# A mixer's second layer in seven block products for eight, with seven accumulators open and its weight sums streamed

## The chip, the core and the metric

The kernel runs on one core of one Trainium2 chip. The core has five engines that run side by side and meet at semaphores: TensorE (PE, matrix products into PSUM), VectorE (DVE), ScalarE (ACT), GpSimd (POOL) and SyncE (SP, which here issues the DMAs). PSUM has eight banks of 128 x 512 fp32; only PE, DVE and ACT reach it here. The metric is device time in microseconds of one execution.

## What is computed

The reference, cut to what matters. The first stage is a causal attention with decay; its output goes, rearranged, into a mixer of two parts.

```python
def _attn_ref(q, k, v, f):              # 8 x 8 heads, 576 tokens, 64 wide
    scores = np.matmul(q, k.transpose(0, 1, 3, 2)) / np.sqrt(64)
    cum = np.cumsum(np.log(np.clip(f, 0.0001, 1.0)), axis=-1)
    scores = np.where(causal, -1e9, scores + cum[:, :, :, None] - cum[:, :, None, :])
    ...
    return np.matmul(attn, v)           # attn: softmax of scores

def _moe_ref(x, U, V, w_ch1, w_ch2):    # x: 8 x 576 x 512
    h = x.transpose(0, 2, 1) @ U @ V
    u = x + h.transpose(0, 2, 1)
    ch = np.maximum(u @ w_ch1, 0.0) @ w_ch2     # 512 -> 2048 -> 512
    return u + ch
```

The two layers of `ch` are most of the arithmetic: 4608 tokens, each through 512 x 2048 and 2048 x 512 weights.

## The kernel before

**Precision.** Every fp32 operand of these layers is held as a high part `h` (rounded to what TensorE multiplies) and a low part `l`, the rest. One product is three matmuls: high by high, low by high, high by low. A matmul has a stationary operand of 128 x 128 (loaded by LDWEIGHTS) and a moving one of up to 512 columns.

**Sweeps.** The 2048 hidden units are 16 chunks of 128. The first sweep goes through attention, mixing and the first six chunks (`NA`), batch by batch; it stores the tokens `u` (to `ud`, high and low) and the sum so far (to `accd`) in HBM. The second sweep takes the other ten chunks (`NB`), whose weights then lie in SBUF: `b1h`, `b1l`, `b2h`, `b2l`. They are read and decoded from raw 64-bit words at the end of the first sweep (`wb_unit`, L976; `decode`, L52: mostly DVE instructions on SBUF).

**Groups.** The second sweep has nine groups of 512 tokens: eight batches and one of the batches' last 64 tokens. Group 0 runs chunk by chunk (`first`, L1034, 12 matmuls of 512 columns; `second`, L1046, 12 matmuls of 512 columns), while the sums of weights and tokens for the rest are made on DVE. Groups 1 to 8 run in five *pairs* of chunks (`pair_of_chunks`, L1151). The first layer of a pair is a 2 x 2 block product (two halves of the 512 model columns, two chunks, two halves of the tokens), done in seven block products for eight, after Strassen and Winograd: `product` (L1143) is six matmuls of 256 columns into a PSUM bank, and DVE forms the sums of products (`plus`, L1167), each reading a bank. The operands are sums too: `weight_sums` (L1089), once, and `token_sums` (L1120, eight DVE instructions of 512 columns per group, from `un`, the next group's tokens) with `token_part` (L1138, ACT the high part, DVE the low).

`relu` (L1029) then makes the hidden units' high part (ACT) and low part (DVE). The second layer is not in block products: `second` adds 3 matmuls of 512 columns to one of four open banks `O` per quarter of the tokens; the last one adds the bank to the group's accumulator in `xn` (L1058) and stores it.

**Order.** In groups 1 to 8 PE and DVE keep the order in which the program is written (`manual_schedule`); the other engines' order comes from a planner that works with estimated times. PE's order is written out so that the second layer of the pair before (`ready`) fills the time in which the first layer's sums are made:

```python
        m5 = product(bank(psF, "F", 5), S1, T1)
        renewed(3)
        plus(s4, m5, s2)
        step()
        go(3)
```

All loads and stores go through SP's queue, in order. Tokens have two buffers (`load_u`, L1020; the next group's 2 MB are asked for at the start of a group). A name in a row of the profile is that of the tile without its number: `M` a bank of the first layer, `O` one of the second, `sum` the tiles of `tmp`, `bh` and `bl` hidden units, `sr` raw weights, `Th` and `Tl` the sums of tokens.

Of the kernel before, what the change touches and what calls it, by code (L numbers as in the profile page):

```python
# [21 lines left out]
P = 128  # L22
# [19 lines left out]
def tile_decay_attention_moe(ctx, tc, qk, v, f, U, V, w1, w2, out):  # L42
# [4 lines left out]
    accd = nc.dram_tensor("accd", (NG, NM, P, DM), F32, kind="Internal").ap()  # L47

# [927 lines left out]
    def wb_unit(i, r):  # L976
        t = stp.tile([P, 1024], I32, tag="raw", name=f"sr{i}{r}")
        if r:
            nc.sync.dma_start(t, w1_src(NA + i))
            h, l = (x[i].rearrange("p c f -> p (c f)") for x in (b1h, b1l))  # L980
        else:
            nc.sync.dma_start(t, w2_src(NA + i))
            h, l = b2h[i], b2l[i]

        a = xn[(B - 3) % NX][:, (2 * i + r) % NM].bitcast(I32)
        decode(t.rearrange("p (n t) -> p n t", t=2), a, h, l, nc.scalar, sub=nc.vector)

# [24 lines left out]

    pool = pools(left, "left")
    up = pool("up", 2)
# [3 lines left out]
    HT = MAIN // 2  # L1018

    def load_u(g):  # L1020
        t = up.tile([P, 2, NDC, MAIN], F32R, tag="u", name=f"u{g}")
        for x in range(2):
            nc.sync.dma_start(t.bitcast(F32)[:, x], ud[g, :, x])
        return t[:, 0], t[:, 1]

    def hidden(name):
        return hp_.tile([P, MAIN], F32R, tag="hh", name=f"bh{name}"), hp_.tile([P, MAIN], F32R, tag="hl", name=f"bl{name}")

    def relu(h, src, cols):  # L1029
        hh, hl = h[0][:, cols], h[1][:, cols]  # L1030
        nc.scalar.activation(hh, src, AF.Relu)  # L1031
        nc.vector.scalar_tensor_tensor(hl, src, 0.0, hh.bitcast(F32), op0=ALU.max, op1=ALU.subtract)

    def first(g, u, i):  # L1034
# [7 lines left out]
        h = hidden(f"{g}_{i}")  # L1042
        relu(h, ps, slice(0, MAIN))
        return h

    def second(z, i, h, x):  # L1046
# [10 lines left out]
        g, o = z["g"], z["acc"][:, x]  # L1057
        nc.vector.tensor_tensor(o, po, o, op=ALU.add)  # L1058
        if g < B:
            nc.sync.dma_start(out[g, P * x : P * x + P], o)  # L1060
        else:
            nc.sync.dma_start(out[2 * x + 1, MAIN:S], o[0:64])
            nc.sync.dma_start(out[2 * x, MAIN:S], o[64:128])
# [6 lines left out]
    for i in range(NB // 2):  # L1070
        blocks = []
        for x in range(3):
# [5 lines left out]
            blocks.append([y.rearrange("p (c f) -> p c f", c=2) for y in pair])  # L1078
        SW.append(blocks)
    Th = sf.tile([P, 4, 2, HT], F32R, tag="uh", name="Th")  # L1080
    Tl = sf.tile([P, 4, 2, HT], F32R, tag="ul", name="Tl")
    tmp = [sf2.tile([P, 2, HT], F32, tag="ost", name=f"sum{x}") for x in range(2)]
    tmp.append(sf.tile([P, 2, HT], F32, tag="TS", name="sum2"))
    tmp = [t[:, y] for t in tmp for y in range(2)]
# [4 lines left out]
    def weight_sums(i, tmp=tmp):  # L1089
        def whole(dst, r, c):  # L1090
            h, l = block(i, r, c)
            nc.vector.tensor_tensor(dst, h.bitcast(F32), l.bitcast(F32), op=ALU.add)

        def diff(dst, x, y, op=ALU.subtract):
            nc.vector.tensor_tensor(dst, x, y, op=op)

        t = [x.rearrange("p (c f) -> p c f", c=2) for x in tmp]
        S1, (S2, S3, S4) = block(i, 1, 0), SW[i]

        def part(dst, src):  # L1100
            split(*dst, src, nc.scalar, nc.vector)

        return [
            lambda: whole(t[0], 1, 0),
            lambda: whole(t[2], 0, 0),
            lambda: diff(t[4], t[2], t[0]),
            lambda: part(S3, t[4]),
            lambda: whole(t[1], 1, 1),
            lambda: diff(t[0], t[0], t[1], ALU.add),
            lambda: part(S1, t[0]),  # L1110
            lambda: diff(t[1], t[0], t[2]),
            lambda: part(S2, t[1]),
            lambda: whole(t[3], 0, 1),
            lambda: diff(t[3], t[3], t[1]),
            lambda: part(S4, t[3]),
        ]

    whole_u = xn[2][:, 0:4].rearrange("p q (c t) -> p q c t", c=2)

    def token_sums(u):  # L1120

        def whole(q):
            c, t = 2 * (q // 2), HT * (q % 2)
            h, l = (x[:, c : c + 2, t : t + HT].bitcast(F32) for x in u)
            nc.vector.tensor_tensor(whole_u[:, q], h, l, op=ALU.add)

        def diff(dst, x, y):
            nc.vector.tensor_tensor(dst, x, y, op=ALU.subtract)

        b11, b12, b21, b22 = (whole_u[:, q] for q in range(4))  # L1130
        return [
            lambda: whole(0), lambda: whole(1),
            lambda: diff(b11, b12, b11), lambda: whole(3),
            lambda: diff(b12, b22, b12), lambda: whole(2),
            lambda: diff(b22, b22, b11), lambda: diff(b21, b21, b22),
        ]

    def token_part(q):  # L1138
        split(Th[:, q], Tl[:, q], whole_u[:, q], nc.scalar, nc.vector)

    T1, T3, T4, T2 = ([x[:, q] for x in (Th, Tl)] for q in range(4))

    def product(ps, a, b):  # L1143
# [5 lines left out]
        return ps  # L1149

    def pair_of_chunks(z, u, i, ready, renew, steps, many):  # L1151

        def go(k):
            for fn in ready[:k]:
                fn()
            del ready[:k]

        def ub(c, t):  # L1160
            return [x[:, 2 * c : 2 * c + 2, HT * t : HT * t + HT] for x in u]

        def bank(pool, tag, k):
            return pool.tile([P, 512], F32, tag=tag, name=f"M{k}_{g}_{i}")[:, 0:HT]

        def plus(dst, ps, other):
            nc.vector.tensor_tensor(dst, ps, other, op=ALU.add)  # L1167

        def step():
            for fn in steps[:many]:  # L1170
                fn()
            del steps[:many]

        def renewed(q):
            if renew:
                token_part(q)

        g = z["g"]
        S1, (S2, S3, S4) = block(i, 1, 0), SW[i]
        h = [hidden(f"{g}_{2 * i + r}") for r in range(2)]  # L1180
        lo, hi = slice(0, HT), slice(HT, MAIN)
        s1, s2, s3, s4, c11, c22 = tmp
        m1 = product(bank(psF, "F", 1), block(i, 0, 0), ub(0, 0))
        nc.scalar.copy(s1, m1)
        m6 = product(bank(psX, "X", 6), S2, T2)
        plus(s2, m6, s1)
        m5 = product(bank(psF, "F", 5), S1, T1)
        renewed(3)
        plus(s4, m5, s2)
        step()  # L1190
        go(3)
        m2 = product(bank(psX, "X", 2), block(i, 0, 1), ub(1, 0))
        plus(c11, m2, s1)
        renewed(0)
        m7 = product(bank(psF, "F", 7), S3, T3)
        plus(c22, m7, s4)
        plus(s3, m7, s2)
        relu(h[0], c11, lo)
        step()
        go(3)  # L1200
        plus(s3, product(bank(psX, "X", 4), block(i, 1, 1), T4), s3)
        relu(h[1], c22, hi)
        renewed(1)
        step()
        plus(s4, product(bank(psX, "X", 3), S4, ub(1, 1)), s4)
# [99 lines left out]
```

## Time and profile before

| | us |
|---|---|
| median of 3 runs (lowest, highest) | 1232.79 (1232.65, 1232.98) |
| the profiled execution | 1233.62 |
| its span, first to last instruction | 1231.8 |
| matmuls O of the second layer in the second sweep, 1080 in all, in the chain of work that ended last | 20% of the span |
| matmuls M of the first layer, groups 1 to 8, in the same chain | 16% |
| DVE busy in 700 to 800 us | 93.08 of 100 |

The profile gives each engine's busy time, the same in stretches, groups of instructions by line of the program, and the chain of work that ended last, followed back from the last instruction. A row of the time line has its start, its duration, the engine, the line, the operation and its tiles; in square brackets stands how long the engine had been idle before it and who ended that. Durations of matmuls are longer than their distance, because they are pipelined: 280 ns each, but some 118 ns from start to start.

### The profile page before, as it was taken

The numbers are of one execution on the slowest core, as the hardware profiler recorded it, in microseconds if no ns is written. First come the engines' busy times: TensorE is split into PE (matmuls) and PEld (weight loads), VectorE is DVE, ScalarE is ACT, GpSimd is POOL, SyncE is SP. The second block draws the span as 40 slices with busy tenths as digits, with TensorE's granted clock in tenths as the row PEclk, the third lists the DMA queues.
The fourth block names the chain that finished last, engine by engine and source line by source line (L and its number), as shares of the span: only waits on it lengthen the run. The fifth ranks groups of instructions, "written<-read, shape, count | busy, mean of one in ns | idle before, by whom it ended". The sixth has DMA issues, their size and how long they took to land.

```text
span 1231.8 us, 21702 instructions
## 1 busy us (share of the span) xinstructions
PE 1201.3 (98%) x7705; PEld 1069.6 (87%) x7705; DVE 896.6 (73%) x2311; ACT 648.9 (53%) x1731; POOL 322.9 (26%) x306
## 2 busy tenths in 40 slices
PE   8999999999999999999999899999999999999998
PEld 6878898988889989989989788888988988898887
DVE  8886888778778777787786799886556555655653
ACT  7787777768767668777675444332122221222211
POOL 3565654444544444444441000000000000000000
PEclk9999999999999999999999999999999999999999
DMA  6546136235325325335342346122130311213010
GB/s 198 151 133 175 51 103 181 76 83 156 89 70 175 106 58 161 99 90 154 87 120 70 115 153 231 35 69 84 55 137 1 137 68 70 103 35 137 1 35 35
DMA packets 67275, 125.85 MB, mean 102 GB/s; under 512 B 7096, under 2 KB 31672, under 8 KB 65120
## 3 DMA queue, kind: packets, MB, share of 16 engines
q1 hardware_dynamic: 67168, 124.47, 33.0%
q8 instruction: 61, 1.00, 0.3%
q14 instruction: 46, 0.38, 0.1%
HBM read 88.66 MB, written 35.78 MB: 101 GB/s over the span
## 4 chain that ended last, share of the span: by engine, by line
PE 83%; DVE 10%; ACT 3%; issue 2%; DMA 1%; POOL 1%; ACTq 0%; DVEq 0%; POOLq 0%
PE O L1054 20%; PE M L1147 16%; PE A L737 10%; PE B L755 9%; PE V L586 5%; PE T L462 4%; PE S L361 3%; PE Hb L1040 2%; PE S L362 2%; PE V L543 1%; PE Tt L646 1%; PE S L358 1%; PE Tu L688 1%; PE St L361 1%; DVE xn L675 1%
## 5 line engine op out<-in xcount | busy, mean ns | idle before, releaser
L1167 DVE TENSOR_TENSOR sum<-M,sum 128x256 f32<-128x256 f32 x280 | 114.7, 422 | 161.0 <-PE M L1147 159.8
L1031 ACT ACTIVATE bh<-sum 128x256 fp32r<-128x256 f32 x160 | 66.8, 419 | 257.5 <-DVE sum L1167 257.5
L390 ACT ACTIVATE P<-S,nm 128x128 f32<-128x128 f32 (+3 forms) x256 | 136.4, 534 | 61.9 <-DVE nm L382 57.6
L382 DVE CUSTOM_DVE_ANT_0 S<-S,mask 128x128 f32<-128x128 f32 (+3 forms) x256 | 125.5, 496 | 45.2 <-PE S L362 36.6
L1054 PE MATMUL O<-b2h,bh 128*128 128x512 f32 x360 | 142.7, 396 | 0.0
L1054 PE MATMUL O<-b2l,bh 128*128 128x512 f32 x360 | 142.2, 395 | 0.0
L1054 PE MATMUL O<-b2h,bl 128*128 128x512 f32 x360 | 141.6, 393 | 0.0
L737 PE MATMUL A<-uh,w1h 128*128 128x256 f32 (+1 forms) x384 | 120.3, 313 | 2.8 <-DVE hl L741 2.8
L737 PE MATMUL A<-ul,w1h 128*128 128x256 f32 (+1 forms) x384 | 113.5, 296 | 0.0
L737 PE MATMUL A<-uh,w1l 128*128 128x256 f32 (+1 forms) x384 | 113.5, 295 | 0.0
L315 POOL CAST G<-qk 64x576 fp32r<-64x576 f32 x52 | 34.9, 672 | 250.0 <-PE St L362 153.7
L755 PE MATMUL B<-w2h,hh 128*128 128x512 f32 x216 | 90.3, 418 | 2.2 <-DVE hl L741 1.2
L462 PE MATMUL T<-ident,P 128*128 128x128 f32 x544 | 87.4, 276 | 0.0
L755 PE MATMUL B<-w2l,hh 128*128 128x512 f32 x216 | 85.0, 394 | 0.0
L755 PE MATMUL B<-w2h,hl 128*128 128x512 f32 x216 | 84.6, 392 | 0.0
L1054 PEld LDWEIGHTS O<-b2l,bh 128*128 128x128 f32 x360 | 67.6, 188 | 16.4
L440 DVE TENSOR_TENSOR PT<-T,PT 128x512 fp32r<-128x512 f32 (+1 forms) x156 | 79.4, 528 | 2.3 <-ACT PT L437 0.6
L586 PE MATMUL V<-PT,VS 128*128 128x448 f32 (+2 forms) x416 | 79.6, 333 | 0.0
L1054 PEld LDWEIGHTS O<-b2h,bl 128*128 128x128 f32 x360 | 67.9, 189 | 11.2
L1054 PEld LDWEIGHTS O<-b2h,bh 128*128 128x128 f32 x360 | 67.9, 189 | 10.6
L737 PEld LDWEIGHTS A<-uh,w1h 128*128 128x128 f32 x384 | 72.9, 190 | 4.5 <-DVE hl L741 4.3
L331 POOL TENSOR_TENSOR G<-qk,G 64x576 fp32r<-64x576 f32 x52 | 74.5, 1433 | 8.5 <-ACT G L315 7.1
(230 smaller groups left out, 3420.5 us busy)
## 6 DMA issues: line engine op xcount, KB each, us to landing
qk<-in_qk_dram SPq DMA_DIRECT2D x104, 288.0 KB
u<-ud SPq DMA_DIRECT2D x16, 1024.0 KB
sr<-in_w_dram SPq DMA_DIRECT2D x20, 512.0 KB
vr<-in_v_dram SPq DMA_DIRECT2D x32, 256.0 KB
accd<-ost SPq DMA_DIRECT2D x32, 256.0 KB
xn<-accd SPq DMA_DIRECT2D x8, 1024.0 KB
out_dram<-xn SPq DMA_DIRECT2D x32, 256.0 KB
ud<-uh SPq DMA_DIRECT2D x7, 1024.0 KB
```

Of the source, the lines that this page charges most:

```text
L331: em.tensor_tensor(g[own, 1, cols], q[own], gf[own, 0, cols], op=ALU.subtract)
L382: nc.vector.tensor_tensor_reduce(ps[:, :w], ps[:, :w], mask[:, 512 - w : 512], scale=-SCALE, scalar=3.0e38, op0=ALU.add, op1=ALU.min, accu ...
L390: nc.scalar.activation(pt, ps[:, :w], AF.Exp, bias=z["nm"][:, col : col + 1], scale=-1.0, accum_out=z["sm"][:, col : col + 1])
L440: defer(2, lambda: nc.vector.tensor_tensor(dstl, src, dsth.bitcast(F32), op=ALU.subtract))
L462: nc.tensor.transpose(tp[:, P * x : P * x + P], z["P"][j][i][:, P * c : P * c + P], ident)
L586: nc.tensor.matmul(pv[:, X0 + lo : X0 + S], VS[:, c, j], pt[:, j, OC[c] + lo - P * c : OC[c] + S - P * c], start=x == 0 and c == 0, stop=F ...
L737: nc.tensor.matmul(ps[:, :nt], wt[:, fc, c], ut[:, c, sl], start=m == 0, stop=m == 3 * NDC - 1)
L755: nc.tensor.matmul(ps, ht[:, fc, P * x : P * x + P], wt[:, fc], start=fc == 0 and m == 0, stop=fc == NA - 1 and m == 2,)
L1031: nc.scalar.activation(hh, src, AF.Relu)
L1054: nc.tensor.matmul(po, ht[:, P * x : P * x + P], wt_[i], start=k == 0 and m == 0, stop=k == NB - 1 and m == 2)
L1147: nc.tensor.matmul(ps, a[x][:, c], b[y][:, c], start=m == 0, stop=m == 5)
L1167: nc.vector.tensor_tensor(dst, ps, other, op=ALU.add)
```

## The change

- **Second layer.** For a pair it too becomes a 2 x 2 block product (two chunks, two halves of the 512 output columns, two halves of the tokens) in seven block products: `product2`, six matmuls of 256 columns. Each product index has an accumulator of its own, open over the five pairs of a group: seven PSUM banks. The sums of products are formed once per group, in `drain`.
- **First layer.** One bank (`FA`) is left for it. A *step* is two products in the two halves of the bank; ACT copies the bank to SBUF (`mc`), and DVE forms the sums from there. The hidden units' sums (`middle`, `last_sum`, `plain_part`) are new, as operands of the second layer.
- **Weights.** The sums of the second layer's weights are made on POOL with ACT during the decoding (`weight_sums2`), stored in HBM (`twd`), and three of four are loaded again for each pair (`load_t`); the fourth is put over a part of `b2h`, `b2l`.
- **Moved.** From group 1 on the token sums and half of the token low parts run on POOL; sums for the first layer's pairs 3 and 4 run on POOL, pair 4 in group 1. Tokens have one buffer `un` and three further tiles (`direct`) for the blocks that are used as they are. They are loaded at pair 1, `direct` in the last pair. ACT too keeps the program's order in groups 1 to 8.

The core of the diff:

```diff
+    twd = nc.dram_tensor("twd", (NB // 2, 4, P, DM), F32, kind="Internal").ap()
...
         decode(t.rearrange("p (n t) -> p n t", t=2), a, h, l, nc.scalar, sub=nc.vector)
+        if i % 2 and not r:
+            weight_sums2(i // 2)
...
+    def weight_sums2(i):
+        eng = nc.gpsimd
+        rows = xn[(B - 2) % NX]
+        w11, w12, w22, w21 = (rows[:, x // 2, 256 * (x % 2) : 256 * (x % 2) + 256] for x in range(4))
...
+        whole(w11, 1, 1)
+        whole(w12, 1, 2)
+        eng.tensor_tensor(w11, w12, w11, op=ALU.subtract)
+        whole(w22, 2, 2)
+        eng.tensor_tensor(w12, w22, w12, op=ALU.subtract)
+        eng.tensor_tensor(w22, w11, w22, op=ALU.subtract)
+        whole(w21, 2, 1)
+        eng.tensor_tensor(w21, w21, w22, op=ALU.add)
+        for x, src in enumerate((w11, w12, w22, w21)):
+            t = rows[:, 2 + x % 2]
+            r = t.bitcast(F32R)
+            split(r[:, 0:256], r[:, 256:512], src, nc.scalar, eng)
+            nc.sync.dma_start(twd[i, x], t)
...
+    def load_t(i, key):
+        nc.sync.dma_start(slots[key].bitcast(F32), twd[i, "1324".index(key)])
+
+    def token_sums(eng):
...
+        for q in range(4):
+            eng.tensor_tensor(whole_u[q], whole_u[q], low_u[q], op=ALU.add)
+        b11, b12, b21, b22 = whole_u
+        diff(low_u[0], b12, b11)
+        diff(low_u[1], b22, b12)
+        diff(low_u[3], b22, low_u[0])
+        diff(low_u[2], b21, low_u[3])
...
+            if i % 2 and i < NB - 1:
+                for fn in weight_sums(i // 2, *((scrap[0:5], nc.vector) if i < 6 else (scrap[5:10], nc.gpsimd))):
+                    fn()
+            if i == NB - 3:
+                token_sums(nc.vector)
...
+    J1, J2 = (1, 6, 5, 2, 7, 4, 3), (4, 1, 5, 6, 7, 2, 3)
...
+        if j == 6:
+            tt(new("2"), m[6], m[1])
+        elif j == 5:
+            tt(new("4"), m[5], s["2"])
+        elif j == 2:
+            tt(new("c11"), m[2], m[1])
+        elif j == 7:
+            tt(new("c22"), m[7], s["4"])
+            tt(new("c21"), m[7], s["2"])
+        elif j == 4:
+            tt(s["c21"], m[4], s["c21"])
+        elif j == 3:
+            tt(new("c12"), m[3], s["4"])
...
+        return act, lambda: tt(k.f[name][1], k.s[key], k.f[name][0].bitcast(F32), ALU.subtract, eng if k.i < NPC - 1 else nc.vector)
+
+    def middle(k):
...
+        def act():
+            nc.scalar.activation(s["c21"], s["c21"], AF.Relu)
+
+        def dve():
+            s["S1"] = fresh()
+            nc.vector.scalar_tensor_tensor(s["S1"], s["c11"], 0.0, s["c21"], op0=ALU.max, op1=ALU.add)
+            s["S2"] = fresh()
+            nc.vector.scalar_tensor_tensor(s["S2"], s["c22"], 0.0, s["S1"], op0=ALU.max, op1=ALU.subtract)
+            nc.vector.scalar_tensor_tensor(s["c21"], s["c22"], 0.0, s["c21"], op0=ALU.max, op1=ALU.subtract)
...
+    AFTER = {
+        2: [(1, lambda k: relu_part(k, "c11", 4))],
+        7: [(1, lambda k: relu_part(k, "c22", 1))],
+        4: [(1, middle), (2, lambda k: plain_part(k, "S1", 5)), (2, lambda k: plain_part(k, "S2", 6)),
+            (2, lambda k: plain_part(k, "c21", 7, nc.gpsimd))],
+        3: [(1, lambda k: relu_part(k, "c12", 2)), (1, last_sum), (2, lambda k: plain_part(k, "S4", 3, nc.gpsimd))],
+    }
...
+    def product2(k, j):
+        ps = acc_ps[j]
+        f, w = k.f[j], operand2(k.i, j)
+        for x in range(2):
+            for m, (a, b) in enumerate(((0, 0), (1, 0), (0, 1))):
+                nc.tensor.matmul(
+                    ps[:, HT * x : HT * x + HT], f[a][:, P * x : P * x + P], w[b],
+                    start=k.i == 0 and m == 0 and x == 0, stop=k.i == NPC - 1 and m == 2, skip_group_check=True,
+                )
+        if j in (4, 6, 7) and (k.n, k.i) != (NG - 1, NPC - 1):
+            load_t((k.i + 1) % NPC, {6: "2", 7: "3", 4: "4"}[j])
+
+    def drain(n, j):
...
+        def rest(blk, t):
+            tt(blk, t, blk, eng=nc.gpsimd)
+
+        if j == 4:
+            tt(C21, ps, C21)
+        elif j == 1:
+            nc.scalar.copy(u, ps)
...
+        elif j == 5:
+            tt(C12, ps, C12)
+            tt(C22, ps, C22)
+        elif j == 6:
+            tt(u6, ps, u)
...
+                tt(C21, ps, C21)
+                tt(C22, ps, C22)
+                rest(C21, u6)
+                rest(C22, u6)
+            store(acc_of(n), (0, 1))
...
+        items = [(n, i, j) for n in range(1, NG) for i in range(NPC) for j in J1]
...
+            batch, items = items[:2], items[2:]
+            if batch:
+                ps = (XA, XB, FB)[s] if s < 3 else FA
+                for x, (n, i, j) in enumerate(batch):
+                    product1(ps[:, HT * x : HT * x + HT], i, j)
...
+                mc = MC[s % 4]
+                nc.scalar.copy(mc, ps)
...
+            todo = [fn(k) for fn, k in later.pop(s, [])]
+            for act, dve in todo:
+                if act:
+                    act()
+            for act, dve in todo:
+                dve()
+            for n, j in drains:
+                drain(n, j)
+            drains = []
+            for n, i, j in batch:
+                if i == NPC - 1 and n + 1 < NG:
+                    if j in direct:
+                        load_direct(order[n + 1], j)
+                    else:
+                        token_part(j, nc.gpsimd)
+                if i == 1 and j == J1[0] and n + 1 < NG:
+                    load_u(order[n + 1])
+                if i == 2 and j == J1[0] and n + 1 < NG:
+                    token_sums(nc.gpsimd)
...
+            for _ in range(2):
+                if queue and queue[0][3] <= s:
+                    n, i, j, _at = queue.pop(0)
+                    product2(pairs[(n, i)], j)
+                    if i == NPC - 1:
+                        drains.append((n, j))
+            s += 1
```

More of the change, by code (lines that the diff above doesn't have):

```diff
@@ L1069, in tile_decay_attention_moe @@
     SW = []
-    for i in range(NB // 2):
+    for i in range(NPC):
         blocks = []
@@ L1077, in tile_decay_attention_moe @@
                 pair = [more[y // 4][:, 256 * (y % 4) : 256 * (y % 4) + 256] for y in (k, k + 1)]
[L1078 removed]
+            blocks.append([halves(y) for y in pair])
         SW.append(blocks)
[L1080 to L1083, printed above, removed]
@@ L1138, in token_part, with one, two, three @@
[L1138 to L1143, printed above, removed]
+            split(*dst, src, nc.scalar, eng)
+        def one():
+            whole(t[0], 1, 0)
+            whole(t[2], 0, 0)
+            diff(t[4], t[2], t[0])
+            whole(t[1], 1, 1)
+        def two():
+            part(S3, t[4])
+            diff(t[0], t[0], t[1], ALU.add)
+        def three():
+            part(S1, t[0])
+            diff(t[1], t[0], t[2])
+            whole(t[3], 0, 1)
@@ new lines, in tile_decay_attention_moe @@
+    TQ = {5: 0, 7: 1, 4: 2, 6: 3}
+    order = [B - 1, *range(B - 2), B, B - 2]
+    load_u(order[1])
+    for j in DIRECT:
+        load_direct(order[1], j)
+    z = {"g": order[0], "acc": xn[1], "po": [None] * NM, "done": [0] * NM}
+    ready = []
+    with tc.manual_schedule(engines={ET.PE}):
+        for i in range(NB):
+            h = first(order[0], cur, i)
+            for fn in ready:
+                fn()
+            ready = [lambda x=x, i=i, h=h: second(z, i, h, x) for x in range(NM)]
+            if i % 2 and i < NB - 1:
+                for fn in weight_sums(i // 2, *((scrap[0:5], nc.vector) if i < 6 else (scrap[5:10], nc.gpsimd))):
+                    fn()
+            if i == NB - 3:
+                token_sums(nc.vector)
@@ L1148, in product @@
                 m += 1
[L1149 to L1205, printed above, removed]
-        renewed(2)
-        go(len(ready))
-        relu(h[1], s3, lo)
-        relu(h[0], s4, hi)
-        step()
-        for r, y in ((0, 0), (0, 1), (1, 2), (1, 3), (1, 0), (1, 1), (0, 2), (0, 3)):
-            ready.append(lambda r=r, y=y: second(z, 2 * i + r, h[r], y))
@@ L1250, in tile_decay_attention_moe, with tt, __init__ @@
-    with tc.manual_schedule(engines={ET.PE}):
-        u, ready = group(0, order[0], cur, [])
-    with tc.manual_schedule(engines={ET.PE, ET.DVE}):
-        for n in range(1, NG):
-            u, ready = group(n, order[n], u, ready)
-        for fn in ready:
-            fn()
+    def tt(dst, x, y, op=ALU.add, eng=nc.vector):
+        eng.tensor_tensor(dst, x, y, op=op)
+    class Pair:
+        def __init__(self, n, i):
+            self.n, self.i = n, i
+            self.m, self.s, self.f = {}, {}, {}
```

275 lines of the change are left out of this document (186 added, 89 removed).

## The prediction

> **What bounds the kernel now.** I read the page's totals first, then the table of stretches, then the chain of work in order of time.
>
> ```profile
> span 1231.8 us, 21702 instructions
> ...
> PE 1201.3 (98%) x7705; PEld 1069.6 (87%) x7705; DVE 896.6 (73%) x2311; ACT 648.9 (53%) x1731; POOL 322.9 (26%) x306
> ...
> POOL 3565654444544444444441000000000000000000
> ```
> ```profile
> 700.00:800.00 100.00, 96.82 (x470) 81.61 (x471) 93.08 (x189) 38.91 (x75) 0.00 (x0) 1.00 0.42 148
> ...
> 900.00:950.00 50.00, 50.00 (x315) 44.94 (x314) 30.01 (x70) 12.44 (x29) 0.00 (x0) 1.00 0.23 85
> ```
> ```profile
> 841.82 2.14 PE M L1147 x18
> 843.96 2.09 PE O L1054 x9
> 846.05 1.42 PE M L1147 x12
> 847.47 2.10 PE O L1054 x9
> 849.57 1.42 PE M L1147 x12
> 850.99 1.40 PE O L1054 x6
> 852.39 2.13 PE M L1147 x18
> ```
>
> TensorE is busy 98% of the span. In the second sweep it never waits: in 900 to 950 us PE is busy all 50 us at full granted clock, while DVE has 30 of 50, ACT 12 and POOL nothing at all. The chain there is a plain alternation of PE groups; nothing else stands in it. One pair of chunks is 42 first-layer matmuls M of 256 columns (2.14 + 1.42 + 1.42 = 4.98 us, 118.5 ns each) and 24 second-layer matmuls O of 512 columns (2.09 + 2.10 + 1.40 = 5.59 us, 233 ns each): 10.57 us, as 841.82 to 852.39 says. Eight groups of five pairs are 40 pairs. So this stage is bound by TensorE alone, and every matmul taken out counts, as long as the other engines can follow. In 700 to 800 us it is different: DVE has 93 of 100 us, and is nearly as full as PE.
>
> **The matmuls.** The second layer of a pair becomes seven products of six matmuls of 256 columns: 42 for 24 of twice the width. No row shows a second-layer matmul of 256 columns; the nearest is M, at 118.5 ns (also with Th and Tl, operands made afresh by ACT and DVE), and half an O is 116.5. I take M's: 42 x 0.1185 = 4.98 us for 5.59. A pair falls from 10.57 to 9.95 us, 0.61 x 40 = **24.4 us less**. The break-even pitch would be 133 ns.
>
> **What DVE must now do.** Per pair it did 7 sums (L1167) and 4 low parts (L1032). It now does 7 sums, 3 low relu parts, 3 instructions of `middle`, 1 of `last_sum` and 2 low parts of `plain_part`: 16, all of 256 columns, and 18 in the last pair of a group.
>
> ```profile
> 1217.29 0.76 DVE L1167 TENSOR_TENSOR sum<-M,sum 128x256 f32<-128x256 f32 x2 [0.29 <-PE M L1147]
> ```
> ```profile
> 716.06 1.29 DVE L69 SCALAR_TENSOR_TENSOR sr<-sr 128x512 f32<-128x512 uint32 x2
> ```
>
> Two in a row take 0.76 us, the single one 0.42, so the pitch is 0.34 us; with 512 columns it is 0.60. 16 x 0.34 = 5.4 of 9.95 us: by time alone DVE has room. So has ACT, with 3.5 copies of a bank (some 0.60 us each) and eight pieces of 256 columns:
>
> ```profile
> L1031 ACT ACTIVATE bh<-sum 128x256 fp32r<-128x256 f32 x160 | 66.8, 419 | 257.5 <-DVE sum L1167 257.5
> ```
>
> 3.5 x 0.60 + 8 x 0.42 = 5.5 us. What changes is where the operands lie. Before, each sum read a PSUM bank. Now ACT copies both products of a step to SBUF (`mc`), and all 16 instructions read two tensors in SBUF. And POOL, idle until now, gets fp32 sums that read SBUF: per group the eight token sums, four low parts (`token_part`), four `rest` of the drain (16 of 512 columns) and two low parts in each of four pairs (8 of 256). The trace has POOL and DVE side by side only in the attention stage:
>
> ```profile
> L630 POOL TENSOR_TENSOR xl<-xn,xh 128x512 fp32r<-128x512 f32 x31 | 40.0, 1291 | 13.6 <-ACT xh L629 12.8
> ...
> L70 POOL TENSOR_TENSOR stg<-stg 128x160 f32<-128x160 f32 x1 | 0.5, 528 | 1.0 <-DMA stg<-in_w_dram 1.0
> ```
> ```profile
> L430 DVE TENSOR_TENSOR sm<-sm x32: 146/826/1416, 15.8 to 655.5; 128x1 f32<-128x1 f32 x32
> ```
> ```profile
> 55.67 1.29 POOL L70 TENSOR_TENSOR stg<-stg 128x512 f32<-128x512 f32 x1 [1.93 <-DVE stg L69]
> ```
> ```profile
> 56.10 0.88 DVE L430 TENSOR_TENSOR sm<-sm 128x1 f32<-128x1 f32 x1
> ```
> ```profile
> 125.52 1.19 DVE L67 SCALAR_TENSOR_TENSOR stg<-stg,xn 128x512 int32<-128x512 int32 x1
> ```
> ```profile
> 37.27 0.45 POOL L632 TENSOR_TENSOR xh<-xn,xh 64x128 fp32r<-64x128 f32 x1
> ```
> ```profile
> 124.78 1.38 POOL L630 TENSOR_TENSOR xl<-xn,xh 128x512 fp32r<-128x512 f32 x1
> 126.23 0.79 POOL L632 TENSOR_TENSOR xh<-xn,xh 64x128 fp32r<-64x128 f32 x1
> ```
> ```profile
> L440 DVE TENSOR_TENSOR PT<-T,PT 128x512 fp32r<-128x512 f32 x52 | 35.6, 685 | 1.1 <-ACT PT L437 0.2
> ```
>
> A POOL sum of 512 columns takes 1.29 us; from 528 ns at 160 columns and 1291 at 512, one of 256 columns is estimated at 0.74. The DVE sum of a single column (L430) takes 0.15 us at best and 0.83 in the median. One instance shows why: it starts at 56.10, while POOL's L70 runs from 55.67 to 56.96, and ends at 56.98. L67, both operands in SBUF, starts at 125.52, lies still until POOL's L630 ends at 126.16 and ends 0.55 later; and POOL's L632, begun at 126.23, waits for it in turn and needs 0.79 us. So the two **take turns, one whole instruction at a time**. Not quite whole: L632 ended 0.31 us after L67 (127.02 against 126.71), though one that waits for nothing takes 0.45 (37.27 us), so some 0.15 us of a POOL instruction can lie beside DVE. L440, with one operand in PSUM, stays at 685 ns in the same stage: such instructions go free, and the old kernel's second sweep was made of them, besides having no POOL work.
>
> [...]
>
> **Where the turns cost time.** A step is two products of each layer, 2.84 us on PE. ACT can copy the bank 1.42 + 0.16 (a matmul's 280 ns less its pitch) after the step's start and needs about 0.60; DVE's 4.6 sums then end at 2.2 + 1.6 = 3.8 us, and ACT takes them up after its next copy, at 2.84 + 2.2 = 5.0. DVE may be late by about 1.2 us; beyond that ACT's next copy is late, the single bank FA is not free, and PE stands. Behind a blocked DVE instruction stand the step's other sums, in order, and the drains.
>
> ```profile
> L177 ACT CAST Th<-xn 128x512 fp32r<-128x512 f32 x22 | 13.6, 617 | 10.8 <-PE M L1147 10.4
> ```
>
> (The copy's 0.60 is from this row of the same size, 617 ns.)
>
> - Pairs 1 and 3: 5.4 + 2 x 0.74 = 6.9 us of 9.95. No cost.
> - Pair 2, with the eight token sums: 5.4 + 1.5 + 8 x 1.29 = 17.2 us (15.7 with 0.15 hidden per turn) for 9.95. Above if all falls into this pair: 7.3 less 1.2 = 6.1 us of stall. Below: spread over pairs 1 to 3 it would be 31.0 of 29.9 us, no stall. I take 3.0, the middle: the sums become ready together, but the last run on into pair 3. **7 groups x 3.0 = 21 us.** Two low parts of the pair before stand behind them in POOL's queue; their product comes late enough that this adds nothing more.
> - Pairs 4 and 0, the boundary: DVE 34 x 0.34 = 11.6, eight drains of 0.60 = 4.8; POOL 2 x 0.74 + 8 x 1.29 = 11.8. With nothing side by side 28.2 us for 19.9; with the drains, which read PSUM, beside POOL and 0.15 hidden per turn, 21.9. Less 1.2: 0.8 to 7.1. I take 2.0, near the lower end because of L440. **7 x 2.0 = 14 us.**
>
> **The front.** In the old kernel DVE decodes the last weights until about 790 us; chunk 9 of b1 has its low part at 781.34 and is read at about 799, b2's of chunk 8 at 789.45 for 799.
>
> ```profile
> 781.34 0.68 DVE L72 TENSOR_TENSOR b1l<-xn,b1h 128x512 fp32r<-128x512 f32 x1
> ...
> 789.45 0.69 DVE L72 TENSOR_TENSOR b2l<-xn,b2h 128x512 fp32r<-128x512 f32 x1
> ```
> ```profile
> 796.00 2.79 PE Hb L1040 x12
> 798.79 2.81 PE O L1054 x12
> ```
>
> Into this stretch `weight_sums2` puts 12 POOL instructions per pair of chunks, and pair 3's sums another 12: 72 x 0.74 = 53 us of POOL, as turns against a DVE that is 93% full and mostly in SBUF. Slack there is 10 to 17 us. Below: 0 (POOL late, decode inside the slack); above: 53 less 6 of idle DVE and some 17 of slack, 30. I take **10**, towards the lower end, since pair 4's sums fall behind the decode. The 20 stores of 256 KB share SP's queue with the loads of raw weights, and wait there for POOL; there is nothing in the old trace for such a store, and its cost is in those two ends.
>
> **Streamed loads.** Three loads of 256 KB per pair (`load_t`) follow the product that frees their slot, and have a pair of time less one product, 9.2 us. The worst place is behind `load_u`:
>
> ```profile
> 851.02 0.80 SPq L1023 DMA_DIRECT2D u<-ud  x2
> ```
> ```profile
> 857.00:858.00 1.00, 1.00 (x10) 1.00 (x10) 0.43 (x1) 0.18 (x1) 0.00 (x0) 1.00 0.62 262
> ```
>
> Those 2 MB are through after 6.6 us, the DMA engines being busy for 0.62 of the last microsecond; a load of 256 KB at their rate (2.1 MB in 6.6 us) adds 0.8. Below: nothing; above: 1.5 us per group, were the 1 MB of `accd` (3.3 us at that rate) ahead of it too: 10.7 for 9.2. I take nothing, as `accd` is asked for a pair earlier. SP's queue also holds the stores, which wait for POOL's `rest`; behind them stand only loads with a pair to spare.
>
> **Filling** the new pipeline (four steps of first layer alone, then one bank) and its end: **2** (0 to 4).
>
> **The sum.** -24.4 + 21 + 14 + 10 + 2 = +22.6 us. The profiled execution took 1233.6 us (span 1231.8): 1256.2. The median of the runs is 0.8 below it: **1255 us**.
>
> **Rivals.**
>
> 1. *The turns fall into DVE's idle time* (faster). Place: pair 2 and the boundary. DVE has 4.5 us per pair to give; POOL wants 26.5 us per group, 5.3 per pair. If the token sums are spread over three pairs and the drains run beside POOL, the stalls are 0 to 10 us in all with a front of 0 to 5: 1233.6 - 24.4 + 0 to 15 = 1209 to 1224. It decides once stalls and front together stay under 24 us, 2.5 us per group and little in front. For it: a group's turns add up to 82 x 0.34 + 8 x 0.74 + 16 x 1.29 = 54.4 us by whole durations, but 50.8 with 0.15 hidden, for PE's 49.8: about even. Against it: they are not even over the pairs. Chance 0.34.
> 2. *Nothing overlaps* (much slower). Stalls near the upper ends, and the front's decode late by 20 to 30 us with SP's queue behind it: 1275 to 1320. For it: DVE's 93% in front. Chance 0.15.
> 3. *The change does not do what it says*: 42 narrow matmuls are no quicker than 24 wide ones. It would need 133 ns where all rows of M have 118. 1233.6 + 47 = 1280. Chance 0.01.
>
> **Chances.** Forecast, 1237 to 1275: 0.45. Rival 1: 0.34. Rival 2 and 3: 0.16. Between, within 0.2% of before (what a measurement of this kernel can tell from no change): 0.05. So faster 0.34, same 0.05, slower 0.61. The range from 1210 to 1292 takes in rival 1 and most of rival 2; the forecast's own is 1237 to 1275.
>
> **What will show it.** Right: matmuls of 256 columns at 118 ns in both layers; DVE instructions of 256 columns with a mean well above 420 ns wherever POOL is busy, near 420 elsewhere; PE idle after DVE or ACT in the third pair of a group and at group ends. Wrong: DVE means near 420 beside POOL would fell the turns; PE idle released by DMA would move the cost to the streamed weights; a PE busy throughout would make it rival 1.

## The result, and the profile after

The changed kernel takes 1315.58 us (median of 4 runs, 1314.56 to 1318.68) against 1232.72 (1232.21 to 1232.98): a ratio of **1.0677 [1.0658, 1.0696]**. Slower was forecast, but 1255 us, with a range that ended at 1292.

The totals and two of the rows of slices on the page of the changed kernel:

```profile
span 1316.6 us, 24582 instructions
...
PE 1213.0 (92%) x8425; PEld 1112.5 (84%) x8425; DVE 1083.0 (82%) x2450; ACT 762.9 (58%) x2019; POOL 630.1 (48%) x571
...
POOL 3665544444444444444312578735364453627322
PEclk9999999999999999999999898898989898989999
```

POOL now works through the second sweep, PE is down from 98 to 92%, and in the second sweep the granted clock falls to 8 tenths again and again. The table of stretches (time on PE, PEld, DVE, ACT, POOL, then PE's clock):

```profile
700.00:800.00 100.00, 87.81 (x405) 73.00 (x404) 93.64 (x149) 35.55 (x71) 60.09 (x51) 0.92 0.55 190
...
900.00:950.00 50.00, 40.26 (x314) 39.66 (x313) 40.32 (x67) 20.09 (x49) 23.15 (x20) 0.90 0.51 158
```

In 700 to 800 us DVE is as busy as before (93.64 against 93.08), with 149 instructions instead of 189: the same kind of work, each instruction longer. That holds for the decode's instructions with one operand in SBUF too, here one form in 700 to 800 us, before and after (count, busy time, mean ns):

```profile
L68 DVE TENSOR_SCALAR sr<-xn 128x512 int32<-128x512 int32 x18 | 7.6, 420 | 0.0
```
```profile
L69 DVE TENSOR_SCALAR sr<-xn 128x512 int32<-128x512 int32 x18 | 11.9, 660 | 0.0
```

The chain of work in order of time, after, at the end of the old stage and in a quiet stretch:

```profile
832.74 2.14 PE px L1258 x18
...
859.69 1.42 PE pf L1258 x12
861.11 1.43 PE po L1355 x12
```

Group 1 starts at 832.74 where it started at 801.60: the front cost 31 us. In the quiet stretch 12 matmuls take 1.42 us in the first layer and 1.43 in the second, 118 to 119 ns each, as forecast. The groups 1 to 8 take 1316.6 - 832.7 = 484 us where they took 430. What PE waits for in them (total, times, longest):

```profile
PE po L1355 <- DVE fx L1262: 26.3, 5, 9.3
PE po L1355 <- DVE frhh L1262: 10.0, 6, 2.2
PE po L1355 <- ACT mc L1426: 8.7, 3, 3.5
```

Most of it is DVE's: 39.8 of 53.2 us in all. One boundary between groups, from the time line; `un` rows are the token sums, `xn<-po` rows the drains:

```profile
893.46 1.85 DVE L1262 TENSOR_TENSOR xn<-mc,xn 128x256 f32<-128x256 f32 x2 [0.74 <-ACT mc L1426]
893.53 5.80 POOL L1181 TENSOR_TENSOR un<-un 128x512 f32<-128x512 f32 x4 [7.65 <-DMA un<-ud]
...
895.24 1.51 DVE L1270 SCALAR_TENSOR_TENSOR frhl<-xn,frhl 128x256 fp32r<-128x256 f32 x1
...
896.67 1.51 DVE L1270 SCALAR_TENSOR_TENSOR frhh<-xn,frhh 128x256 fp32r<-128x256 f32 x1
...
898.11 1.27 DVE L1262 TENSOR_TENSOR xn<-po,xn 128x512 f32<-128x512 f32 x2
...
899.30 5.78 POOL L1178 TENSOR_TENSOR un<-un 128x512 f32<-128x512 f32 x4
```

The eight token sums start when their load has landed, and that is at the boundary, beside the drains, not in pair 2: the planner had put the load ahead too (SP asked for its second half at 885.91). While they run, DVE instructions of 256 columns with both operands in SBUF take up to 1.51 us, nearly one to each POOL instruction of 1.45; the drains, which read PSUM, keep 0.68. The chain goes on from there:

```profile
909.83 1.49 DVE fx L1262
911.32 0.04 issue
911.36 2.71 PE po L1355 x11
914.08 2.56 PE pf L1258 x12
916.63 1.61 PE px L1355 x12
918.25 1.43 PE pf L1258 x12
```

PE had waited 9.34 us until 911.36:

```profile
911.36 0.58 PE L1355 MATMUL po<-b2h,fx 128*128 128x256 f32 x1 [9.34 <-DVE fx L1262]
```

Then groups of twelve matmuls (eleven rows in the first) take 2.71 and 2.56 us instead of 1.43: they run at about half rate (the granted clock was 0.50 from 911.30 to 916.60 us), and 2.6 us more are lost before the full rate is back (1.00 from 922 to 927 us).

### The profile page after: what moved, and what is told of

Read it like the earlier page. It is cut to its first block, busy times and chain, and to the rows that moved or that the text cites. A ratio compares the mean times of both kernels' runs of the same rounds, so it can differ in the third digit from the quotient of the medians.

```text
span 1316.6 us, 24582 instructions
## 1 busy us (share of the span) xinstructions
PE 1213.0 (92%) x8425; PEld 1112.5 (84%) x8425; DVE 1083.0 (82%) x2450; ACT 762.9 (58%) x2019; POOL 630.1 (48%) x571
## 4 chain that ended last, share of the span: by engine, by line
PE 64%; DVE 24%; ACT 4%; issue 4%; DMA 2%; POOL 2%; DVEq 0%; SPq 0%; ACTq 0%; POOLq 0%
PE pf L1258 11%; PE A L738 9%; PE B L756 7%; PE po L1355 7%; PE V L587 5%; DVE xn L1262 5%; PE T L463 3%; PE px L1355 3%; PE S L362 2%; PE S L363 2%; PE pf L1355 2%; DVE frhl L1270 1%; PE V L544 1%; PE Tt L647 1%; PE S L359 1%
## 5 line engine op out<-in xcount | busy, mean ns | idle before, releaser
L1426 ACT COPY mc<-pf 128x512 f32<-128x512 f32 x138 | 81.0, 587 | 189.3 <-PE pf L1258 189.2
L391 ACT ACTIVATE P<-S,nm 128x128 f32<-128x128 f32 (+3 forms) x256 | 136.3, 533 | 61.7 <-DVE nm L383 57.6
L1262 DVE TENSOR_TENSOR xn<-mc,xn 128x256 f32<-128x256 f32 x200 | 135.1, 699 | 44.0 <-ACT mc L1426 42.6
L1262 POOL TENSOR_TENSOR frhh<-xn,frhh 128x256 fp32r<-128x256 f32 x40 | 33.3, 833 | 139.5 <-ACT frhh L1303 139.5
L332 POOL TENSOR_TENSOR G<-qk,G 64x576 fp32r<-64x576 f32 x52 | 74.4, 1431 | 8.5 <-ACT G L316 7.1
L331 POOL TENSOR_TENSOR G<-qk,G 64x576 fp32r<-64x576 f32 x52 | 74.7, 1436 | 3.8
L362 PE MATMUL S<-G 128*128 128x128 f32 x208 | 71.2, 347 | 4.9 <-ACT P L391 2.9
L438 ACT CAST PT<-T 128x512 fp32r<-128x512 f32 (+1 forms) x156 | 67.8, 466 | 11.1 <-PE T L463 10.2
L738 PEld LDWEIGHTS A<-uh,w1l 128*128 128x128 f32 x384 | 73.9, 192 | 0.3
L738 PEld LDWEIGHTS A<-ul,w1h 128*128 128x128 f32 x384 | 73.5, 191 | 0.0
```

What stands on the lines that cost most here:

```text
L362: nc.tensor.matmul(ps, G[j][:, 0, c0 : c0 + P], G[j][:, 2, cols], start=first, stop=False)
L391: nc.scalar.activation(pt, ps[:, :w], AF.Exp, bias=z["nm"][:, col : col + 1], scale=-1.0, accum_out=z["sm"][:, col : col + 1])
L738: nc.tensor.matmul(ps[:, :nt], wt[:, fc, c], ut[:, c, sl], start=m == 0, stop=m == 3 * NDC - 1)
L1262: eng.tensor_tensor(dst, x, y, op=op)
L1426: nc.scalar.copy(mc, ps)
```

## Experiments

Except where an interval is given, a time is one run, beside runs of the kernel before on the same chip at 1232.2 to 1232.8.

**1. POOL's work of the groups 2 to 8 on DVE.** Token sums (one per step, as `token_steps`), low parts (two of group 1's too) and rests; the rest of the front is left.

```diff
-            tt(blk, t, blk, eng=nc.gpsimd)
+            tt(blk, t, blk)
-                    token_sums(nc.gpsimd)
+                    sums_to_do = token_steps()
-                        token_part(j, nc.gpsimd)
+                        token_part(j, nc.vector)
```

> The changed kernel with everything that POOL did for groups 2 to 8 put on DVE: token sums (one per step from the start of pair 2, two in the first step), token low parts, the rests of the drain, the low parts of c21 and S4. The front is as in the changed kernel, and so are the first layer's weight sums of pairs 3 and 4 on POOL. Turns (POOL and DVE lock each other out, whole instruction by whole instruction): DVE has 82 x 0.34 + 8 x 0.34 + 24 x 0.60 = 45.0 us per group for 49.8 of PE, with nobody to wait for; DVE instructions of 256 columns go back from 700 to about 420 ns; groups 1 to 8 fall from 484 us to 410-440, the time to 1240-1272. Rival (the new pipeline with its one bank and DVE's 16 instructions per pair is what stalls, POOL or not): DVE has still more to do, and the time stays at 1316 or rises.

1257.96 us, 57.6 less, as the turns had it. The group of DVE's sums on the page, of the changed kernel and then of this one (count, busy time, mean):

```profile
L1262 DVE TENSOR_TENSOR xn<-mc,xn 128x256 f32<-128x256 f32 x200 | 135.1, 699 | 44.0 <-ACT mc L1426 42.6
```
```profile
L1274 DVE TENSOR_TENSOR xn<-mc,xn 128x256 f32<-128x256 f32 x200 | 80.1, 425 | 25.6 <-ACT mc L1439 22.5
```

With more work on DVE its instructions are back at 425 ns and the kernel is faster. In 900 to 950 us PE is busy throughout:

```profile
900.00:950.00 50.00, 50.00 (x423) 50.00 (x422) 44.73 (x111) 25.27 (x62) 0.00 (x0) 1.00 0.58 185
```

**2. POOL in the written order** (`ET.Pool` added to the engines of `manual_schedule`), so that the token sums stand in pair 2.

> The changed kernel with POOL too in the order in which the program is written, in groups 1 to 8; nothing else differs. In the trace of the changed kernel the planner has the eight token sums run beside the drains at the start of a group, not in pair 2. Place theory: back in pair 2 they cost 3 to 6 us per group instead of adding to the drains; the longest waits of PE (9 us before fx) fall to 3-5; time 1275-1300. If only the number of turns counts, wherever they are: 1310-1320.

1332.89 us, 17 more: both expectations missed. PE's largest wait in the groups, and POOL's time line, show why:

```profile
PE po L1355 <- DVE frhh L1262: 41.7, 7, 7.3
```

```profile
900.06 2.69 POOL L1262 TENSOR_TENSOR xn<-xn,xn 128x512 f32<-128x512 f32 x2 [13.93 <-DVE xn L1262]
...
908.12 5.78 POOL L1181 TENSOR_TENSOR un<-un 128x512 f32<-128x512 f32 x4
913.86 5.68 POOL L1178 TENSOR_TENSOR un<-un 128x512 f32<-128x512 f32 x4
919.50 0.90 POOL L1262 TENSOR_TENSOR frhh<-xn,frhh 128x256 fp32r<-128x256 f32 x1
```

The late rests and the token sums now follow one another with one gap of 0.96 us: from 900 to 920 us POOL has a turn for nearly each of DVE's instructions that read SBUF alone.

**3 and 4. The front, one part each.** In 3 `weight_sums2` runs on DVE (`eng = nc.vector`); in 4 SP's stores write the decoded weights, so that they wait for no sum (the output then lacks these sums).

> The changed kernel with the second layer's weight sums (60 instructions of 256 columns in the front) on DVE instead of POOL; pair 3's and 4's first-layer sums stay on POOL, groups as in the changed kernel. Turns: each POOL instruction kept DVE for about 0.55 us, on DVE itself it takes 0.34; DVE's 256- and 512-column instructions go back to 420 and 685 ns there, SP's queue no longer stands behind POOL; the first product of group 1 comes at 805-822 instead of 831, the time 1288-1308. Rival (DVE is the bound in front, 93% full): 20 us more on DVE make it later still, 833-850, time 1318-1335.

> The changed kernel, but the 20 stores to twd store decoded weights b2h, b2l as they are instead of the sums (the output then lacks the right weight sums): the POOL work is unchanged, but SP's queue no longer waits for POOL before it asks for the next raw weights. Queue theory (the front lost its time because loads of raw weights stood behind stores that waited for POOL, as at 787.8 us): DVE's idle 5.6 us at 787-792 goes, the first product of group 1 comes at 815-825, time 1300-1310. Turns alone: within 4 us of 1315.

1311.87 and 1312.77 us: neither alone does much. 3 missed both of its expectations; 4 missed the queue theory's 1300 to 1310 and fits turns alone. In 3 the first matmul of group 1 came at 808.17, but PE then stood 5.6 us and 15.6 us. Its time line there:

```profile
816.24 5.74 POOL L1181 TENSOR_TENSOR un<-un 128x512 f32<-128x512 f32 x4
...
817.91 1.50 DVE L1146 TENSOR_TENSOR xn<-xn 128x256 f32<-128x256 f32 x1
...
819.34 1.51 DVE L181 TENSOR_TENSOR xn<-xn 128x256 fp32r<-128x256 f32 x1
```

DVE's work met POOL's token sums for the next group, turn by turn. That it was late by what it had taken over is not shown by itself. SP's queue, in 4, is a side matter of 3 us.

**5 to 8. Both together, and their limits.** 5 is 1 and 3; 6 is 1 without second-layer weight sums (the stores write pieces of the decoded weights); 7 has only the token sums on DVE; 8 is 5 with the first-layer sums on DVE too, so that POOL does nothing in the second sweep.

> The two earlier edits together: the sums of groups 2 to 8 on DVE, and the 12 instructions for each pair of second-layer weight sums on DVE too. POOL keeps only the first-layer weight sums of the pairs 3 and 4. The run with the groups on DVE alone took 1257.96 us, that with the front alone on DVE took 1311.87, 3.7 us off. If POOL's turns are what the front loses (my theory), the edit is worth more here than 3.7 us, as no token sums of POOL lie beside DVE's late work any more: 1240 to 1252 us. Rival, that the front loses by the amount of work alone (60 instructions of 0.42 us are 25 us, on whichever engine): 1252 to 1265 us.

> The groups on DVE, and the second-layer weight sums left out altogether: their stores write pieces of the decoded weights instead, so that all transfers stay and the output is not the reference's. It prices the front. If the sums (whoever makes them) are what makes the front 31 us later, the front comes back to within 6 us of before and the time is 1226 to 1236 us. Rival, that the stores and the loads of the streamed weights, or the first matmuls of the new order, make the front late: 1245 us or more.

> Only the eight token sums of each group go to DVE, one per step; the rests of the drains and the low parts stay on POOL. All of them on DVE took 57.6 us off 1315.6. If the token sums, which stand in a block of 11.6 us of turns, make most of it (my theory), 25 to 45 us of that come here: 1270 to 1290 us. Rival, that the rests and low parts at the boundary hold most: 1295 us or more.

> As the run with both on DVE, and the first-layer weight sums of the pairs 3 and 4 too: POOL does no sum after the first sweep. That is 36 instructions more for DVE, about 15 us of its time. If the turns at the front cost more than DVE's own work (my theory), it is 2 to 10 us faster than the run before it in this set that leaves these on POOL; rival, that DVE is the bound of the front and every instruction given to it is paid: 5 to 15 us slower than that run.

1249.84, 1231.08, 1276.12 and 1246.67 us, each time inside the first of its expectations. So the token sums on POOL cost 1315.58 - 1276.12 = **39.5 us**, rests and low parts 1276.12 - 1257.96 = **18.2**, the second-layer weight sums 1257.96 - 1231.08 = **26.9**. In 6 the first group starts at

```profile
808.63 0.28 PE L1251 MATMUL px<-Th,swhh 128*128 128x256 f32 x1
```

7 us later than before, where within 6 was expected. Even with these sums for nothing the kernel would only have come out level: 24.4 us of matmuls bought 1.6.

**9, 11, 12. Number of turns, or their place?** All three are 1 with the token sums on POOL again, in the written order. 9 emits one per step. In 11 a POOL sum of one column ahead of each reads what DVE has just written in the step; in 12 one such gate stands ahead of all eight.

```diff
+    def gate():
+        t = ring[(count["r"] - 1) % len(ring)][:, 0:1]
+        nc.gpsimd.tensor_tensor(Usum[1][:, 0:1], t, t, op=ALU.add)
...
+            if sums_to_do:
+                gate()
+                sums_to_do.pop(0)()
```

> The rests, low parts and rest of POOL's work of groups 2 to 8 on DVE as in the first experiment (1257.96 us), but the eight token sums of a group on POOL again: in the written order now, one per step from the third pair of chunks on, where the changed kernel had them in a block beside the drains. Theory 'clump': a turn costs DVE some 1 us, DVE has 5.4 us to spare in a pair, and the kernel pays where more turns come together than that; spread, they are nearly free: 1255 to 1268 us. Rival 'number': every turn is paid, wherever it lies, and the token sums cost 39.5 us as they did in a block (1315.58 against 1276.12): 1290 us or more.

1302.88 us, which looks like "number". But POOL's time line says that the edit didn't do what it says:

```profile
952.79 11.47 POOL L1192 TENSOR_TENSOR un<-un 128x512 f32<-128x512 f32 x8 [49.11 <-DVE xn L1274]
```

All eight ran in one block, beside the drains: here the order of emission did not hold POOL back once it had its data.

> In the run before, the order of emission did not spread POOL's token sums: POOL waited for the loads and then ran all eight in one block of 11.4 us beside the drains. Here a sum of one column ahead of each token sum reads what DVE has written in this step, so that POOL can make only one per step of 2.85 us, in the third to fifth pairs of chunks, away from the drains. All else on DVE. Theory 'clump' (DVE idles 54% of a quiet step, 1.5 us, and a turn costs it some 1 us, so turns one per step are hidden): within 10 us of the run with everything on DVE, 1253 to 1268 us. Rival 'number' (every turn is paid in full, 0.8 us each as in the block of the run before): 1285 us or more.

> The same with one such gate ahead of all eight token sums: one block of 11.6 us in the third pair of chunks, away from the drains, where my prediction had put it at 3.0 us per group. Theory 'clump': eight turns of 1 us against some 6.3 us of DVE's idle time in the block, and 1.2 us of lateness that PE bears: 1 to 4 us per group, 1265 to 1286 us, between the spread run and the one beside the drains (1302.88). Rival 'number': the same as the spread run within 5 us. If it is near 1303, the drains beside the block were not what made it dear.

1266.05 us spread, 1289.49 in a block in the quiet part (a little above its 1286). POOL's time lines, 12 first:

```profile
909.19 11.43 POOL L1192 TENSOR_TENSOR un<-un 128x512 f32<-128x512 f32 x8
```
```profile
907.01 0.24 POOL L1202 TENSOR_TENSOR xn<-xn 128x1 f32<-128x1 f32 x1 [28.78 <-DVE xn L1333]
907.21 1.48 POOL L1192 TENSOR_TENSOR un<-un 128x512 f32<-128x512 f32 x1
...
915.66 1.49 POOL L1192 TENSOR_TENSOR un<-un 128x512 f32<-128x512 f32 x1
...
927.94 1.56 POOL L1192 TENSOR_TENSOR un<-un 128x512 f32<-128x512 f32 x1
```

The same 56 sums cost, over having them on DVE, 8.1 us one by one (1.2 per group), 31.5 in a quiet block (4.5), 44.9 beside the drains (6.4). So it is not the number: from one by one to a block costs 23.4 us, and from a quiet block to one beside the drains 13.4 more.

**10 and 13. What is left at the boundaries.** 13 is 8 with the four rests of the drains put off, two per step once no drain is due. 10 has a third row for the front's stores as well; that row still held rows of the extra group, which are overwritten in it.

```diff
         def rest(blk, t):
-            tt(blk, t, blk)
+            if last:
+                tt(blk, t, blk)
+            else:
+                late.append(lambda: tt(blk, t, blk))
```

> All sums on DVE (1246.67 us), and two edits of the order: the four rests of a group's drains, and the stores behind them, come after the drains, two per step, and the front's weight sums have three rows for their stores instead of two. PE waits there 9.1 us in all at the group boundaries on DVE and 8.6 us once in the front on a PSUM copy of ACT, whose queue waited for stores. If DVE's lateness at the boundaries is the drains' (my theory), about 7 us of the one and 3 of the other go: 1235 to 1242 us. Rival, that DVE is the bound over the whole group, so that work put off is paid in the next pair: 1244 to 1248 us.

> All sums on DVE (1246.67 us) with the four rests of a group's drains put after them, two per step; the stores of the front keep their two rows. In the run before with both edits PE's waits in the groups fell from 9.1 to 2.7 us, while the third row, which still held rows of the extra group, was wrongly overwritten and shifted the waits of the front. By the drains theory 6 to 7 us go: 1238 to 1242 us. Rival, that the gain of that run was the third row's: 1245 to 1248 us.

1238.69 and 1242.53 us (13 half a microsecond above its 1242). PE's waits in the groups, in 8 and then in 13:

```profile
PE po L1367 <- DVE fx L1274: 4.7, 4, 1.2
PE po L1367 <- DVE frhh L1274: 3.1, 3, 1.1
PE pf L1367 <- DVE xn L1274: 1.3, 3, 0.4
```

```profile
PE po L1368 <- DVE frhh L1274: 2.7, 3, 0.9
```

PE's waits fell by 6.4 us and the time by 4.1. Group 1 began 1.2 us later in 13 (812.02 us for 810.84); the rest of the difference is not assigned.

**14 and 15. Less work in the front.** 14 is 13 with sums made from the decoded numbers before they are split; 15 also makes the low parts two at a time.

```diff
-        whole(w11, 1, 1)
-        whole(w12, 1, 2)
-        eng.tensor_tensor(w11, w12, w11, op=ALU.subtract)
...
+        a2, a1 = (xn[(B - 3) % NX][:, 2 * y % NM] for y in (2 * i, 2 * i + 1))
+        eng.tensor_tensor(w11, a1[:, hi], a1[:, lo], op=ALU.subtract)
```

> The run before, with less work for DVE in the front: the second-layer weight sums read the decoded numbers before they are split, so the four additions of high and low part for each pair go away (20 instructions of 0.415 us, 8.3 us). If the front's loss is the amount of DVE's work (DVE is busy 97% of it), 5 to 9 us go: 1230 to 1236 us. Rival, that it is the order of DVE's and ACT's queues: within 3 us of the run before.

> As the run before, and the low parts of these sums two at a time: 10 instructions of 512 columns (0.68 us) for 20 of 256 (0.415 us), 1.5 us less for DVE, and 10 conversions fewer for ACT, but both rows of a store are in use at once. By the amount of work 1 to 3 us less than the run before; rival, that ACT's wait for the stores grows: 1 to 5 us more.

1233.57 us (ratio to before 1.0008 [0.9998, 1.0017]) and 1233.89 (1.0006 [0.9997, 1.0015]). Taking 8.3 us of DVE's work away took 9.0 us of time: the front is paid by amount. The further 1.5 us of 15 can't be seen, and neither of its expectations held. One wait of PE is left there in both, in 15:

```profile
PE pf L1264 <- ACT mc L1440: 9.3, 1, 9.3
```

**16 and 17. The same work, later.** 16 is 15 with the first-layer weight sums of pairs 2 and 3 made step by step in group 1 (and the load of `accd` a pair later there); in 17 that group's token sums also come a pair later.

```diff
-                steps = weight_sums(NPC - 1, spent[0:5], nc.vector)
+                steps = [fn for y in range(2, NPC) for fn in weight_sums(y, spent[0:5], nc.vector)]
+                steps.pop(0)()
...
-            if steps and s % 2 == 0:
+            if steps:
```

> The run with the wide low parts, with the first-layer weight sums of the pairs 2 and 3 moved out of the front into the first group, one part per step ahead of their use, where those of pair 4 already were. There PE waited 9.3 us once, because DVE made the sums of the pairs 1 to 3, some 18 instructions in a row, ahead of the first group's own sums. If it is the order of DVE's queue, 5 to 9 us go: 1224 to 1229 us. Rival, that DVE has no room in the first group either (it is busy 90% of it): 1231 to 1235 us.

> As the run before, and in the first group the token sums come one pair of chunks later, so that they don't meet the deferred weight sums (by its sums DVE would be 0.4 us behind per step there for seven steps). By the order theory 0 to 3 us less than the run before; rival: the same within 1 us.

1230.14 us (0.9980 [0.9971, 0.9990]) and **1229.44 us (0.9973 [0.9963, 0.9983])**: 17 is faster than both kernels, by 0.3% than the one before. 16 missed its 1224 to 1229 and fell short of the rival's 1231. 17 is 0.7 us below 16, which fits both of its expectations, and the intervals overlap. The wait of 9.3 us shrank to

```profile
PE pf L1264 <- ACT mc L1440: 3.8, 1, 3.8
```

in 17, while DVE's busy time in 820 to 860 us rose from 35.39 to 38.48 of 40: order was worth 4.5 us. That what is left is amount is argued, not shown.

## Why the prediction was wrong, step by step

| term, us | predicted | measured | from |
|---|---|---|---|
| narrow second layer | -24.4 | pitch as predicted | 12 matmuls in 1.42 to 1.43 |
| token sums beside DVE | +21 | +39.5 | changed kernel less 7 |
| boundary: rests, low parts | +14 | +18.2 | 7 less 1 |
| second-layer weight sums in front | +10 | +26.9 | 1 less 6 |
| filling and the rest | +2 | +22.8 | 6 less before, plus 24.4 |
| sum | +22.6 | +82.9 | unrounded terms |

- **The matmuls and the streamed weights** were right: no row of PE's waits in the groups of the changed kernel names a load.
- **The turns** were right as a mechanism: 425 ns alone, 1.5 us beside a POOL instruction of 1.45, 0.68 for drains that read PSUM; moved to DVE, the work is cheaper although DVE has more of it (1257.96 us in 1 for 1315.58). Nor are the turns whole: 0.34 + 1.29 would be 1.63 us a turn, and the boundary shows 1.45, so 0.18 us lies side by side, near the 0.15 that the old trace had shown. That POOL's work beside DVE is the cause in the groups is shown by 1 and 7; that its price hangs on bunching and place, by 9, 11 and 12. But not only instructions with two operands in SBUF were longer: the decode's TENSOR_SCALAR with one took 660 ns for 420, and 419 in 8, where POOL does nothing there.
- **The step that failed is "Where the turns cost time"**, in two ways. It put the token sums into pair 2, as the program has them, though POOL's order was not the written one: they ran beside the drains, and the two stalls that I had priced apart fell on one spot. And between 0 and 6.1 us per group I took 3.0; in place they cost 5.6 (39.5 / 7), and even away from the drains 4.5, inside the prediction's two ends but not at their middle.
- **The front** was sized wrong: 10 taken between 0 and 30 for 72 instructions, 26.9 measured for 60 of them. Its mechanism was right in the smaller part only: with the groups' sums on DVE, moving these sums off POOL too gave 8.1 us (1 less 5), and the other 18.8 (5 less 6) are paid on DVE as well. The sum set turns of POOL against 10 to 17 us of slack; on DVE these 60 instructions are some 25 us (60 x 0.415), so that slack took up about 6. The reason given for the low end, that pair 4's sums fall behind the decode, is not borne out: on DVE, too, that work is paid nearly in full (8.3 us of it gave 9.0).
- **Filling** hid 21 us that had no term: 7 us of a later first group even without these sums, and 9.4 us of waits at the boundaries in 6, where DVE makes its drains and sums alone (13 took most such waits away). The end is 3.8 us longer: from the start of the last matmul to the end of the span it is 8.2 us in 6 (1221.07 to 1229.3) and 4.4 before (1227.38 to 1231.8). Some 2 us are not assigned; 2 were forecast.
- **The clock had no term at all.** The mean granted clock fell from 0.998 to 0.969. Taken as half rate, as in the 0.50 after the wait of 9.34 us, that is some 80 us of the span (an estimate: 2 x 0.031 x 1316.6); part of that is waiting itself (the clock was 0.80 from 900 to 911.30 us, where PE was busy for 1.69 us). In the groups its price can be estimated: beyond the waits, the distances of matmuls above 118.7 ns add up to 24 us on PE's time line, and to 3.5 in 6, whose granted clock was 1.00 in every stretch from 800 to 1200 us. So of the 78 us by which the groups miss 430 - 24.4, 53 are waits, some 20 half rate and 3 the longer end. These 20 lie in the measured terms.
- **The range** treated three terms of one cause as if their errors would cancel. With every term at its own upper end (43, 50, 30 and 4 us) the sum would have been 1336. Rival 2, 1275 to 1320 with stalls near the upper ends, holds the 1315.58 and had too little chance, 0.15; its queue was a side matter.

## What to carry to other kernels

Before work is moved to POOL, list which DVE instructions beside it read SBUF alone: here those of 256 columns with two operands went from 0.42 us to as much as 1.51, and a TENSOR_SCALAR with one from 0.42 to 0.66 in the mean. So a block of POOL work should lie where DVE has slack (the token sums cost 4.5 us per group in 12, for 6.4 beside the drains in 9), or be held back by a real data dependence, one instruction at a time (1.2 in 11); in 9 the order of emission held nothing back. Terms that share one cause go to the upper or the lower end together, and the range has to be their sum. In the front, where DVE was busy 95.67 of 100 us in 700 to 800 us of 8 (96.48 in 14), 8.3 us of its work left out in 14 gave 9.0, so look in such a stretch first for work that can be left out (sums from numbers not yet split) or put off to where they are needed.

## What the chip showed unexpectedly

**POOL can be starved.** At the boundary the two engines alternate almost strictly: from 893.46 to 905.05 us POOL's eight token sums and eight DVE instructions with two operands in SBUF. In the front of the changed kernel they don't:

```profile
778.56 6.42 POOL L1002 TENSOR_TENSOR xn<-b2h,b2l 128x256 f32<-128x256 f32 x1
...
779.07 0.68 DVE L68 SCALAR_TENSOR_TENSOR xn<-xn,sr 128x512 int32<-128x512 int32 x1
779.67 0.68 DVE L70 SCALAR_TENSOR_TENSOR sr<-sr 128x512 f32<-128x512 uint32 x1
```

POOL's sum of 256 columns, 0.90 us at a boundary (905.05), lay 6.42 us while DVE ran instruction after instruction at their normal 0.68. What decides between alternation and starvation stays open.

**A wait of PE can cost more than itself, and its length alone does not decide it.** After 9.34 us the matmuls ran at 214 ns for 118 for some 5 us, at a granted clock of 0.50. In run 12 the clock stayed at 1.00 in 900 to 950 us, though PE waited 2.95 us there. Yet after a shorter wait in the same run, and after one in run 7, matmuls follow at 210 to 220 ns; the first row here is of the stretch that stayed at 1.00, the last of run 7:

```profile
919.10 0.39 PE L1274 MATMUL pf<-d,b1h 128*128 128x256 f32 x1 [2.95 <-ACT mc L1443]
```
```profile
978.46 0.86 PE L1371 MATMUL po<-Tl,frhh 128*128 128x256 f32 x5 [2.57 <-DVE frhh L1286]
...
980.08 0.41 PE L1274 MATMUL pf<-d,b1h 128*128 128x256 f32 x1
980.29 0.63 PE L1274 MATMUL pf<-Th,sw 128*128 128x256 f32 x2
```
```profile
1072.42 0.58 PE L1367 MATMUL po<-b2h,frhh 128*128 128x256 f32 x1 [2.46 <-DVE frhh L1274]
```

So the waits of 2.57 and 2.46 us were followed by about half rate, and the longer one of 2.95 us was not. What decides between two waits of like length stays open.
